# The norm row of q, spread over the partitions by two DMAs through DRAM

## The chip, the core and the metric

The kernel runs on one core of a Trainium2 chip. Its engines work beside each other and meet by semaphores: PE (matmuls; PEld is the load of their weights), DVE (vector), ACT (scalar functions), POOL and SP. SP does nothing here but issue DMAs; POOL issues DMAs and does a little arithmetic. Sixteen DMA engines carry out what both issue; the profile calls SP's queue q1 and POOL's q0. The metric is the device time in microseconds of one execution. Before the change it is 519.28 us, the median of three runs (518.49 to 519.51).

## What is computed

Attention over channels, with each column of q and k divided by its norm, and then a channel mix. B = 4, N = 6208, C = 256, the inner width of the mix is 1024, tau = 1:

```python
qn = q / (np.linalg.norm(q, axis=1, keepdims=True) + 1e-06)
kn = k / (np.linalg.norm(k, axis=1, keepdims=True) + 1e-06)
s = kn.transpose(0, 2, 1) @ qn / tau          # 256 x 256 for each batch
a = softmax(s, axis=-1)
x = v @ a                                     # N x 256
x_prev = x shifted by one row
xk = mu_k * x + (1.0 - mu_k) * x_prev
xr = mu_r * x + (1.0 - mu_r) * x_prev
k = np.maximum(xk @ w_k, 0.0)
out = sigmoid(xr @ w_r) * (k * k @ w_v)
```

The kernel multiplies the raw k and q first and scales the 256 x 256 result: its rows by the inverse norms of k, its columns by the inverse norms of q. A row's factor is one number per partition, which an instruction takes as it is. A column's factor differs along the free dimension and is the same on all partitions: the 256 inverse norms of q have to stand as a row on each of the 128 partitions. This row is what the change is about.

## The kernel before

Batch 0 has a stage of its own at the head (about 40 us). The rest is one pipeline over 48 blocks of 512 rows of v, twelve for each batch, and a last block with the 64 rows that are left of each batch. The outer loop runs over i, from -2 to 48, the inner over j from 0 to 7. One pass of the inner loop is called a slot here, with the number T = 8i + j. Each engine executes its instructions in the order in which the loops emit them; nothing reorders them later. In the steady state a slot emits:

- up(i + 1, j): two matmuls into kT_ps (L336) and the relu on ACT (kr, L339); one slot later DVE squares it (kk, L345)
- down(i, j): three or five matmuls into v_ps (L384); at j = 1 and 5 DVE multiplies a half block with its gate (res, L397), at j = 1 SP stores the block (L400)
- at j = 0, 1, 4, 5 a gate matmul (L355) into the PSUM bank with the tag g, of which there is one; at j = 2 and 6 ACT empties it (L390)
- at j = 0 and 2 x_half(i + 2): x = v @ a for a coming block (L255), which reads a_sb, the softmax of that block's batch, and an ACT copy into X
- at j = 4 the difference delta (L310), at j = 5 and 6 the two halves of xk (L321) for block i + 2, at j = 0 and 1 those of xr
- at j = 1 a DMA transpose of v (vT, L236) on SP, at j = 2 a load of v (L224) on POOL

Beside this, 49 units for each of the batches 1 to 3 are spread over the slots (a table of due slots, `due`). A unit is two matmuls of k with q into s_ps (L423) and a square of the same rows on ACT (L427). take_sum adds squares on DVE (L445, L449); take_norm adds over the partitions with four short matmuls into n_ps (L462), which also lies in bank g, and an ACT copy to ssq (L464). With the last norm of a batch, at j = 7, the pieces of its softmax join the list `chain`, and each slot takes one of them:

- a: the sum of ssq on DVE and the square root on POOL (L163)
- a2: plus 1e-6, and the reciprocal (L168, L170): nrm_o, a tile of 128 x 4, channel p of half h of q at [p, h]
- b1: two DVE products of a diagonal matrix with the inverse norms (dq, L177)
- bcast: an fp32 matmul of ones with dq (L182), which puts the row on all partitions of bank g, and an ACT copy to rq_bc (L492)
- c: s times the row, on DVE (L495)
- e: two exponentials with sums on ACT (L199)
- f: reciprocals and scaling into a_sb on DVE (L203, L204)

A None in the list lets one slot pass. The piece bcast uses bank g, so it is let out at j = 3 or 7 alone, and take_norm is skipped in that slot. By these rules the pieces of batch 1 come at T = 64, 66, 67, 71, 73, 74, 75, and the first x_half that reads the new a_sb at T = 80. The slots of batch 2 are later by 96, those of batch 3 by 192; batch 3 has no units and norms beside its softmax any more.

Batch 0 makes its row with the same functions spread and broadcast, in the stage at the head.

Of the kernel before, what the change touches and what calls it, by code (L numbers as in the profile page):

```python
# [10 lines left out]
F32 = mybir.dt.float32  # L11
# [7 lines left out]
def kernel(  # L19
# [13 lines left out]
    nc = tc.nc  # L33
    B, N, C = q.shape
    D = C
    DF = moe_w_k.shape[1]
    P = 128
# [13 lines left out]
    pq = ctx.enter_context(tc.tile_pool(name="pq", bufs=4))  # L51
    pn = ctx.enter_context(tc.tile_pool(name="pn", bufs=2))
    p2 = ctx.enter_context(tc.tile_pool(name="p2", bufs=3))
    ps = ctx.enter_context(tc.tile_pool(name="ps", bufs=1, space=bass.MemoryType.PSUM))
    ctx.enter_context(tc.manual_schedule())

# [99 lines left out]
    def root(src, n):  # L156
        a = pn.tile([P, 4], F32, name="nrm_a")
        if len(src.shape) == 3:
            nc.vector.tensor_reduce(a[:, :n], src, axis=AX, op=OP.add)
        else:  # L160
            nc.vector.tensor_copy(a[:, :n], src)
        r = pn.tile([P, 4], F32, name="nrm_r")
        nc.gpsimd.tensor_tensor(r[:, :n], a[:, :n], half[:, :n], op=OP.pow)  # L163
        return r

    def inverse(r, n):

        nc.vector.tensor_scalar_add(r[:, :n], r[:, :n], 1e-6)  # L168
        o = pn.tile([P, 4], F32, name="nrm_o")
        nc.vector.reciprocal(o[:, :n], r[:, :n])  # L170
        return o


    def spread(r):
        dq = pn.tile([P, 2, P], F32, name="dq", bufs=1)
        for h in range(2):
            nc.vector.tensor_scalar_mul(dq[:, h], ident_f, r[:, h:h + 1])  # L177
        return dq

    def broadcast(dq, tag, **kw):  # L180
        bc_ps = ps.tile([P, C], F32, name="bc_ps", tag=tag, **kw)
        nc.tensor.matmul(bc_ps, ones_f, dq.rearrange("p h d -> p (h d)"), start=True, stop=True)  # L182
        return bc_ps
# [7 lines left out]
    def soft_half(b, ih, t_sb, rk, e_sb, sm, mx):  # L191

        if SHIFT:
            nc.vector.tensor_scalar_mul(t_sb[:, ih], t_sb[:, ih], rk[:, ih:ih + 1])
            nc.vector.tensor_reduce(mx[:, ih:ih + 1], t_sb[:, ih], axis=AX, op=OP.max, negate=True)
            nc.scalar.activation(e_sb[:, ih], t_sb[:, ih], AF.Exp, bias=mx[:, ih:ih + 1],
                                 accum_out=sm[:, ih:ih + 1])
        else:
            nc.scalar.activation(e_sb[:, ih], t_sb[:, ih], AF.Exp, scale=rk[:, ih:ih + 1],  # L199
                                 accum_out=sm[:, ih:ih + 1])  # L200

    def soft_scale(b, ih, e_sb, sm):
        nc.vector.reciprocal(sm[:, ih:ih + 1], sm[:, ih:ih + 1])  # L203
        nc.vector.tensor_scalar_mul(a_sb[:, b, ih, :], e_sb[:, ih], sm[:, ih:ih + 1])  # L204

    def soft_tiles():
        return (pn.tile([P, 2, C], F32, name="t_sb"), pn.tile([P, 2, C], F32, name="e_sb"),
                pn.tile([P, 2], F32, name="sm"), pn.tile([P, 2], F32, name="mx"))
# [24 lines left out]
    def v_transpose_dma(i):  # L233
        v_bf = st.pop((i, "v"))
        vT = new_vT(i)
        nc.sync.dma_start_transpose(vT.rearrange("p s h t -> p (s h) t"), v_bf.rearrange("p s c -> p (s c)"))  # L236
# [105 lines left out]
    def square(i, fh):  # L342
        m = size(i)
        kr = st.pop((i, "kr", fh))
        nc.vector.tensor_tensor(st[i, "kk"][:, fh, :m], kr[:, :m], kr[:, :m], op=OP.mult)  # L345

    def gate_mm(i, s):
        if s * P >= size(i):
            return
        if s % 2 == 0:  # L350
            st[i, "g", s // 2] = ps.tile([P, 2, D], F32, name="g_ps", tag="g")
        g_ps = st[i, "g", s // 2]
        xr = st[i, "xr"]
        for dh in range(2):
            nc.tensor.matmul(g_ps[:, s % 2], xr[:, dh, s * P:(s + 1) * P], w_r_sb[:, dh, :],  # L355
                             start=s % 2 == 0 and dh == 0, stop=dh == 1, skip_group_check=True)
# [30 lines left out]
    def gate_act(i, u):  # L387

        if (i, "g", u) in st:
            nc.scalar.activation(st[i, "res"][:, 2 * u:2 * u + 2], st.pop((i, "g", u)), AF.Tanh, scale=0.5)  # L390
# [45 lines left out]
    norms = []  # L436
# [38 lines left out]
    def softmax_pieces(b):  # L475
        t_sb, e_sb, sm, mx = soft_tiles()
        hold = {}

        def a():
            hold["n"] = root(ssq[b], 4)  # L480

        def a2():
            hold["r"] = inverse(hold["n"], 4)
            if inv_tau != 1.0:
                nc.vector.tensor_scalar_mul(hold["r"][:, 2:], hold["r"][:, 2:], inv_tau)

        def b1():
            hold["dq"] = spread(hold["r"])

        def bcast():  # L490
            hold["bc"] = pn.tile([P, C], F32, name="rq_bc", bufs=1)
            nc.scalar.copy(hold["bc"], broadcast(hold["dq"], "g"))  # L492

        def c():
            nc.vector.tensor_tensor(t_sb, s_sb[b], hold["bc"].unsqueeze(1).to_broadcast([P, 2, C]), op=OP.mult)  # L495

        def e():
            for ih in range(2):
                soft_half(b, ih, t_sb, hold["r"][:, 2:], e_sb, sm, mx)

        def f():
            for ih in range(2):
                soft_scale(b, ih, e_sb, sm)

        return [a, None, a2, b1, None, bcast, None, c, e, f]


    order = [("q", NB)] + [("q", g) for g in range(LEAD)]
# [71 lines left out]
    chain = []  # L580
    lst = {}

    for i in range(-2, NBLK):
        for j in range(8):
            T = i * 8 + j
            if i == LAST - 1 and j == 7:

                st[LAST, "res"] = pq.tile([P, S, D], F32, name="res", tag="f4", bufs=NF)
                for s in range(2):
                    gate_mm(LAST, s)  # L590
                gate_act(LAST, 0)
            if j in (2, 6):
                gate_act(i, j // 4)
            if 0 <= i + 1 < NBLK:
                up(i + 1, j)
            if j == 0 and i >= 0:
                square(i, 7)
            if j > 0 and 0 <= i + 1 < NBLK:
                square(i + 1, j - 1)
            if j == 5:  # L600
                finish(i, 0)
            if j == 1:
                finish(i - 1, 1)
            if i >= 0:
                if j in (0, 1, 4, 5) and i < LAST:
                    gate_mm(i, j // 4 * 2 + j % 4)
                down(i, j)
            n = i + 2
            if n == 0 and j == 0:
                x_first()  # L610
            if 0 < n < LAST:
                if j == 0:
                    x_half(n, 0)
                if j == 2:
                    x_half(n, 1)
            if n < NBLK:
                if j == 4:
                    mix_delta(n)
                if j in (5, 6) and n > 0:
                    mix(n, "xk", j - 5)  # L620
            if j in (0, 1) and 0 <= i + 1 < NBLK:
                mix(i + 1, "xr", j)
            if j == 7 and 2 <= i + 3 < NPE:
                v_transpose_pe(i + 3, st.pop((i + 3, "v")), 0, S, "v")
            if j == 1 and NPE <= i + 5 < LAST:
                v_transpose_dma(i + 5)
            if j == 2 and NPE < i + 7 < LAST:
                v_load(i + 7)
            bank_g = False
            if chain and (chain[0] is None or chain[0].__name__ != "bcast" or j in (3, 7)):  # L630
                f = chain.pop(0)
                if f is not None:
                    f()
                    bank_g = f.__name__ == "bcast"
            if bank_g:
                pass
            elif j in (3, 7) or j in (2, 6) and len(norms) > 1:
                take_norm()
            if j in (2, 3, 6, 7) or len(sums) > 2:
                take_sum()  # L640
            for u in due.get(T, []):
                b, g, s = units[u]
                at = (b - 1) * (NB + 1) + GORD.index(g)
                more_rows(at + 4)
                unit(b, g, s)
                if g == GORD[-1] and s == S - 1:
                    evac_s(b)
            if i >= 0 and i // NB < B:
                bl = i // NB
                if i % NB == 2 and j == 1:  # L650
                    lst["v"] = left_load(bl)
                if i % NB == 4 and j == 3:
                    lst["t"] = left_transpose(lst["v"])
                if i % NB == 6 and j == 4:
                    left_x(bl, lst["t"])
# [35 lines left out]
```

## Time and profile before

| | |
|---|---|
| median of three runs | 519.28 us |
| the profiled execution | 519.07 us |
| its span, first to last instruction | 517.3 us |
| bc_ps on PE, L182 (three pairs in the pipeline, one at the head) | 380 ns each |
| dq on DVE, L177 | 282 ns each |
| rq_bc on ACT, L492 | 372 ns, three |
| c on DVE, L495 | 685 ns, three |
| e on ACT, L199 | 506 ns each, and 191 for the sum |
| DMA packets | 143202, 83.51 MB |

How to read the profile: the busy share of an engine is an average over the span. A timeline has one line for each instruction, or for some of the same kind in a row: start, duration, engine, source line, operation, what is written and read, and in brackets how long the engine had been idle before it and what it had waited for. Instructions of an engine overlap, so that a matmul of 0.38 us can be followed after 0.22; the distance of starts is what one costs in a full stream. An issue of a DMA says nothing of its end; that is in the DMA view, as the time to landing.

### The profile page before, as it was taken

The numbers are of one execution on the slowest core, as the hardware profiler recorded it, in microseconds if no ns is written. First come the engines' busy times: TensorE is split into PE (matmuls) and PEld (weight loads), VectorE is DVE, ScalarE is ACT, GpSimd is POOL, SyncE is SP. The second block draws the span as 40 slices with busy tenths as digits, with TensorE's granted clock in tenths as the row PEclk, the third lists the DMA queues.
The fourth block names the chain that finished last, engine by engine and source line by source line (L and its number), as shares of the span: only waits on it lengthen the run. The fifth ranks groups of instructions, "written<-read, shape, count | busy, mean of one in ns | idle before, by whom it ended". The sixth has DMA issues, their size and how long they took to land. (4 is left out here: it accounts for less than half of the span.)

```text
span 517.3 us, 10260 instructions
## 1 busy us (share of the span) xinstructions
PE 496.5 (96%) x3770; PEld 340.4 (66%) x3770; DVE 451.2 (87%) x895; ACT 434.7 (84%) x830; POOL 104.1 (20%) x145
## 2 busy tenths in 40 slices
PE   5789899999999999999999999999999999999996
PEld 2464676776667767667666667767666666666675
DVE  3467899999999999999999999999989888888884
ACT  6777899998999899899999899899787777777773
POOL 0036623322341131131251132100031000000000
PEclk9999999999999999999999999999999999999999
DMA  8989999999999999799899999963297653432123
GB/s 311 407 286 185 194 189 205 193 215 169 189 184 194 174 185 148 125 181 168 103 178 214 173 172 153 157 126 81 62 180 130 131 114 88 101 84 80 55 70 101
DMA packets 143202, 83.51 MB, mean 161 GB/s; under 512 B 51184, under 2 KB 139824, under 8 KB 143152
## 3 DMA queue, kind: packets, MB, share of 16 engines
q0 software_dynamic: 65808, 33.01, 52.3%
q1 hardware_dynamic: 77184, 49.72, 38.4%
q8 instruction: 29, 0.48, 0.4%
q10 hardware_dynamic: 160, 0.13, 0.1%
q14 instruction: 21, 0.17, 0.1%
HBM read 78.71 MB, written 25.43 MB: 201 GB/s over the span
## 5 line engine op out<-in xcount | busy, mean ns | idle before, releaser
L339 ACT ACTIVATE kr<-kT_ps 128x512 bf16<-128x512 f32 (+1 forms) x392 | 232.4, 595 | 37.1 <-PE kT_ps L336 29.5
L336 PE MATMUL kT_ps<-xk,w_k_sb 128*128 128x512 bf16 (+1 forms) x784 | 231.3, 377 | 1.1 <-DVE xk L321 1.0
L384 PE MATMUL v_ps<-w_v_sb,kk 128*128 128x256 bf16 x1536 | 230.4, 273 | 0.0
L345 DVE TENSOR_TENSOR kk<-kr 128x512 bf16<-128x512 bf16 (+1 forms) x392 | 162.1, 418 | 36.5 <-ACT kr L339 33.0
L384 PEld LDWEIGHTS <-kk 128*128 128x128 bf16 x1536 | 150.2, 98 | 57.6
L427 ACT ACTIVATE sq<-qk 128x512 f32<-128x512 bf16 (+1 forms) x147 | 93.0, 633 | 1.1 <-DMA qk<-in_k_dram 1.1
L336 PEld LDWEIGHTS <-w_k_sb 128*128 128x128 bf16 x784 | 74.8, 98 | 22.2 <-issue 1.0
L355 PE MATMUL g_ps<-w_r_sb,xr 128*128 128x256 bf16 x388 | 73.8, 272 | 1.2 <-ACT ssq L464 1.1
L257 ACT CAST X<-xT_ps 128x512 bf16<-128x512 f32 x94 | 55.5, 591 | 20.5 <-PE xT_ps L255 19.8
L321 DVE SCALAR_TENSOR_TENSOR xr<-delta,mu_r_t,X 128x512 bf16<-128x512 bf16 x96 | 71.6, 746 | 0.0
L321 DVE SCALAR_TENSOR_TENSOR xk<-delta,mu_k_t,X 128x512 bf16<-128x512 bf16 x94 | 70.2, 746 | 0.0
L355 PEld LDWEIGHTS <-xr 128*128 128x128 bf16 x388 | 37.9, 98 | 48.2 <-issue 4.8
L397 DVE SCALAR_TENSOR_TENSOR res<-res,v_ps 128x512 f32<-128x512 f32 x96 | 65.4, 681 | 0.0
L413 POOL DMA_DIRECT2D qk<-in_q_dram x39 | 28.7, 735 | 164.1 <-ACT sq L427 142.6
L390 ACT ACTIVATE res<-g_ps 128x512 f32<-128x512 f32 x97 | 57.8, 596 | 0.4 <-PE g_ps L355 0.4
L423 PE MATMUL s_ps<-qk 128*128 128x256 bf16 (+1 forms) x294 | 56.1, 272 | 1.7 <-DMA qk<-in_k_dram 1.7
L255 PE MATMUL xT_ps<-vT,a_sb 128*128 128x512 bf16 x188 | 55.9, 379 | 0.2 <-ACT X L282 0.2
L224 POOL DMA_DIRECT2D v_bf<-in_v_dram x48 | 37.3, 779 | 52.4 <-DMA vT<-v_bf 46.9
L445 DVE TENSOR_TENSOR sq<-sq 128x1024 f32<-128x1024 f32 x36 | 43.9, 1220 | 1.0 <-ACT sq L427 1.0
L423 PEld LDWEIGHTS <-qk 128*128 128x128 bf16 (+1 forms) x294 | 26.7, 97 | 14.3 <-DMA qk<-in_k_dram 2.3
L310 DVE TENSOR_TENSOR delta<-X 128x1024 bf16<-128x1024 bf16 x48 | 33.0, 687 | 0.1
L413 POOL DMA_DIRECT2D qk<-in_k_dram x39 | 28.9, 742 | 7.0 <-DMA w_v_sb<-in_moe_w_v_dram 2.1
(72 smaller groups left out, 233.4 us busy)
## 6 DMA issues: line engine op xcount, KB each, us to landing
out_dram<-res SPq DMA_DIRECT2D x48, 512.0 KB, 3.3
v_bf<-in_v_dram POOLq DMA_DIRECT2D x48, 256.0 KB, 8.1
qk<-in_q_dram POOLq DMA_DIRECT2D x36, 256.0 KB, 8.7
qk<-in_k_dram POOLq DMA_DIRECT2D x36, 256.0 KB, 9.3
f<-in_q_dram SPq DMA_DIRECT2D x12, 512.0 KB, 8.5
f<-in_k_dram SPq DMA_DIRECT2D x11, 512.0 KB, 9.3
vT<-v_bf SPq DMA_TRANSPOSE x44, 7.0
w_k_sb<-in_moe_w_k_dram POOLq DMA_DIRECT2D x1, 512.0 KB, 6.0
```

The source lines that it names most:

```text
L255: nc.tensor.matmul(xT_ps, a_sb[:, b, ih, dh * P:(dh + 1) * P], vT[:, :, ih, :], start=ih == 0, stop=ih == 1)
L321: nc.vector.scalar_tensor_tensor(o[:, dh], st[i, "d"][:, dh], mu[:, dh:dh + 1], X[:, dh, c:c + M], op0=OP.mult, op1=OP.add)
L336: nc.tensor.matmul(kT_ps[:, :m], w_k_sb[:, dh, fh * P:(fh + 1) * P], xk[:, dh, :m], start=dh == 0, stop=dh == 1)
L339: nc.scalar.activation(kr[:, :m], kT_ps[:, :m], AF.Relu, scale=RH)
L345: nc.vector.tensor_tensor(st[i, "kk"][:, fh, :m], kr[:, :m], kr[:, :m], op=OP.mult)
L355: nc.tensor.matmul(g_ps[:, s % 2], xr[:, dh, s * P:(s + 1) * P], w_r_sb[:, dh, :], start=s % 2 == 0 and dh == 0, stop=dh == 1, skip_group_ ...
L384: nc.tensor.matmul(v_ps[:, s % 2], kk[:, fh, s * P:(s + 1) * P], w_v_sb[:, fh, :], start=s % 2 == 0 and fh == 0, stop=fh == 7, skip_group_ ...
L390: nc.scalar.activation(st[i, "res"][:, 2 * u:2 * u + 2], st.pop((i, "g", u)), AF.Tanh, scale=0.5)
L397: nc.vector.scalar_tensor_tensor(r, r, 1.0, st.pop((i, "v", u)), op0=OP.add, op1=OP.mult)
L413: nc.gpsimd.dma_start(qk[:rows, :n, i], src_rows(t, b, g))
L423: nc.tensor.matmul(cov[b][:, ih, :], qk[:rows, s, 1, ih * P:(ih + 1) * P], qk[:rows, s, 0, :], start=g == GORD[0] and s == 0 and ih == 0, ...
L427: nc.scalar.activation(G["sq", s // 2][:rows, s % 2], qk[:rows, s], AF.Square)
```

## The change

For batches 1 to 3 the row is no longer made by the diagonal and the matmul. One DMA on SP writes the 256 inverse norms of q from SBUF to a tile in DRAM, and another reads them back, with a stride of 0 over the partitions, into rq_bc. The pieces b1 and bcast are replaced by these two, in successive slots, and eight None stand between the second and c. The rule that held bcast for j = 3 or 7 and skipped take_norm goes with it. By the list, the pieces of batch 1 come at T = 64, 66, 67 (bcast_out), 68 (bcast_in), 77 (c), 78 (e) and 79 (f). The head of the kernel is not touched.

```diff
+    pd = ctx.enter_context(tc.tile_pool(name="pd", bufs=2, space=bass.MemoryType.DRAM))
...
-        def b1():
-            hold["dq"] = spread(hold["r"])
-
-        def bcast():
+        def bcast_out():
+            hold["d"] = pd.tile([2, P], F32, name="rq_d")
+            with nc.allow_non_contiguous_dma(reason="256 words"):
+                nc.sync.dma_start(hold["d"].rearrange("h p -> p h"), hold["r"][:, 0:2])
+
+        def bcast_in():
             hold["bc"] = pn.tile([P, C], F32, name="rq_bc", bufs=1)
-            nc.scalar.copy(hold["bc"], broadcast(hold["dq"], "g"))
+            nc.sync.dma_start(hold["bc"], hold["d"].rearrange("h p -> (h p)").unsqueeze(0).to_broadcast([P, C]))
...
-        return [a, None, a2, b1, None, bcast, None, c, e, f]
+        return [a, None, a2, bcast_out, bcast_in] + [None] * 8 + [c, e, f]
...
-            bank_g = False
-            if chain and (chain[0] is None or chain[0].__name__ != "bcast" or j in (3, 7)):
+            if chain:
                 f = chain.pop(0)
                 if f is not None:
                     f()
-                    bank_g = f.__name__ == "bcast"
-            if bank_g:
-                pass
-            elif j in (3, 7) or j in (2, 6) and len(norms) > 1:
+            if j in (3, 7) or j in (2, 6) and len(norms) > 1:
                 take_norm()
```

## The prediction

> **What bounds the kernel now.** I read the shares of the span first, then the windows around the three places where the row is made, then the timelines of PE, ACT and DVE there, and last the DMA view of the same stretches. The shares, and two windows (columns: PE, PEld, DVE, ACT, POOL busy, clock, DMA share, GB/s):
>
> ```profile
> PE 496.5 (96%) x3770; PEld 340.4 (66%) x3770; DVE 451.2 (87%) x895; ACT 434.7 (84%) x830; POOL 104.1 (20%) x145
> 140.00:165.00 25.00, 24.53 (x184) 16.99 (x183) 24.31 (x51) 22.98 (x49) 10.59 (x14) 1.00 1.26 198
> 165.00:255.00 90.00, 90.00 (x674) 62.57 (x672) 84.97 (x159) 81.74 (x161) 18.79 (x26) 1.00 1.02 156
> ```
>
> PE never rests between the row of batch 1 and that of batch 2 (90.00 of 90), so what PE is spared or made to wait at a row moves the end by as much, if DVE (94% there, 97% at the row) can follow. The timeline at the row of batch 1, PE first, then ACT:
>
> ```profile
> 147.72 0.60 PE L182 MATMUL bc_ps<-dq,ones_f 128*128 128x256 f32 x2
> 148.15 0.38 PE L423 MATMUL s_ps<-qk 128*128 128x256 bf16 x2
> ...
> 153.68 0.59 PE L336 MATMUL kT_ps<-xk,w_k_sb 128*128 128x512 bf16 x2
> 154.75 0.38 PE L355 MATMUL g_ps<-w_r_sb,xr 128*128 128x256 bf16 x2 [0.47 <-ACT ssq L464]
> ...
> 153.57 0.50 ACT L199 ACTIVATE e_sb<-t_sb,nrm_o 128x256 f32<-128x256 f32 x1
> 153.97 0.19 ACT L199 ACTIVATION_READ_ACCUMULATOR e_sb<-t_sb,nrm_o 128x1 f32 x1
> 154.06 0.58 ACT L339 ACTIVATE kr<-kT_ps 128x512 bf16<-128x512 f32 x1
> 154.54 0.16 ACT L464 COPY ssq<-n_ps 128x4 f32<-128x4 f32 x1
> ```
>
> Two losses are seen. The broadcast holds PE from 147.72 to 148.15, 0.43 us. Then the two exponentials (1.0 us of ACT) push back the ssq copy, which must clear bank g before the gate matmul; that starts 1.07 us after the up matmul in front of it, where 0.43 is usual: 0.64 lost. Batch 2 shows both again (265.51; 271.47 to 272.54). Batch 3, with no rows left to sum, differs:
>
> ```profile
> 387.60 0.16 DVE L203 RECIPROCAL sm<-sm 128x1 f32<-128x1 f32 x1 [0.82 <-ACT e_sb L199]
> ...
> 391.25 0.39 PE L336 MATMUL kT_ps<-xk,w_k_sb 128*128 128x512 bf16 x1
> 392.25 0.38 PE L336 MATMUL kT_ps<-xk,w_k_sb 128*128 128x512 bf16 x1 [0.60 <-DVE xk L321]
> ```
>
> DVE waits for the exponentials, its xk comes late, and PE's second matmul starts 1.00 after its first instead of 0.22: 0.78 lost. There too the copy of the row (382.50 to 382.87) holds bank g until 382.92: 0.62 in place of 0.43, 0.19 lost.
>
> **The queues.** SP's timeline, then lines from the DMA view of windows 140.5 to 142 (vT), 150 to 156 (out_dram) and 150.83 to 154.4 (q0):
>
> ```profile
> 141.09 1.69 SPq L236 DMA_TRANSPOSE vT<-v_bf  x1
> 150.83 0.37 SPq L400 DMA_DIRECT2D out_dram<-res  x1
> ...
> vT<-v_bf SPq DMA_TRANSPOSE x1, 8.6
> ...
> out_dram<-res SPq DMA_DIRECT2D x1, 512.0 KB, 7.4
> ...
> q0 software_dynamic: 1409, 0.70, 145.5%
> ```
>
> The transpose lands at 141.09 + 8.6 = 149.7. The store issued at 150.83 has not one packet on q1 until 154.4: POOL's seven loads, issued from 140.86 to 145.31, have the engines to themselves. Elsewhere the same store lands in 3.1.
>
> **What the Trainium skill says.** All on the page "DMA: Bandwidth & Descriptors". "Rules for kernel authors": a non-contiguous last dim makes one descriptor per element, so bcast_out is 256 of 4 bytes. The trace has the like: the two loads of mu (256 words each) fall in window 33 to 34.2, where 500 of 662 packets are under 512 B. "Two DMAs through the same engine are not ordered": the reader has to wait for the writer's semaphore on the issuing engine, so SP stands still between the two. No run here shows that yet. "Anatomy of one DMA": about 2.0 us fixed, mostly the write's receipt, HBM the slowest, plus bytes at 436 GB/s; for 512 KB that makes an estimate of 3.2, and the quiet store shows 3.1. "Queues, rings and completion order": ring order inside a row, and turns between rows packet by packet. The trace agrees on the first (q1 carries the store's packets, then the transpose's) and not quite on the second: the store's first turn came after 3.6 us.
>
> **The change, part by part.** A slot is one pass of the inner loop, T = 8i + j; times are batch 1's.
>
> 1. Removed: per batch two diagonal products on DVE (0.40), one fp32 matmul pair on PE (0.43), one ACT copy (0.27 net) that had waited 0.38 for PE. PE's 0.43 lies on the path. DVE's and ACT's shares lie beside PE and count only as room.
> 2. Moved: take_norm is no longer pushed out of slot 71, so the norm of slot 75 (a pair of short matmuls and the ssq copy) is done at 71, with no exponential near it. c, e, f go from slots 73, 74, 75 to 77, 78, 79. The 0.64 at slot 76 is gone.
> 3. What is late next: x_half of block 12 reads a_sb in slot 80, straight behind f. PE's slot 76 now starts at 153.25, slot 77 at 154.23, slot 80 at 157.70. kr of slot 76 is ready at 153.25 + 0.59 + 0.60 = 154.45; DVE then does kk 0.34, res 0.60, first xk 0.66, and c could start at 156.05, ending by 156.74. The second xk is ready at 157.73; PE asks for it at 157.92, 0.2 to spare. ACT is done with kr of slot 78 at 156.82, with the exponentials at 157.81, the next kr 158.3 and ssq (the norm of slot 79) at 158.5. The gate matmul wanted bank g at 158.13, so a new wait of 0.41. f ends on DVE at 158.95 to 159.0; x_half, pushed by the same wait, wants its second half at 159.31: hidden. Without that cover it would cost 0.3.
> 4. Batches 1 and 2: -0.43 - 0.64 + 0.41 = -0.66 each. Batch 3 by the same steps: -0.43 - 0.19 - 0.78, then c ahead of the second xk costs 0.42 and f ahead of x_half 0.29: -0.69.
> 5. Added on SP: bcast_out (issue 0.43, as mu) at 142.8, behind the transpose in q1, so its packets pass at 149.4. Nobody else needs SP until 150.83; in batch 3 the store and transpose of 384.61 wait some 2 us, which three blocks of lead hide. Landing of bcast_out: no row for words written to DRAM. Lower end 0.3 (the transpose's own tail), upper 3.0 (2.0 fixed by the skill, plus an estimate of 1.0 for 16 slow writes per engine); I take 0.8, since a quiet 512 KB store leaves little room for more: 150.2. bcast_in issues at 150.3; first packet after 3.6 as the store's (0.9 if the queue were quiet): 153.9; 128 packets of 1 KB at the store's rate (105 in 0.8 us) 1.0, landing 0.4: 155.3. c wants it at 156.05. Margin 0.75, cost nothing. If the cover is gone, c stands at the head of DVE, and xk, kk and PE are late by about what is missing. Batch 3: transpose landed 385.8, row out 386.2, issued at 386.3 and back some 2.5 later, between the 1.4 + 0.9 of a quiet queue and the 4.4 that the store of 384.61 takes, at 388.8, c at 389.45.
>
> Sum: 2 x -0.66 - 0.69 = -2.0. Profiled execution: 519.07 (span 517.3 and 1.8 around it) - 2.0 = 517.1. That execution is 0.21 under the median of 519.28, inside the spread of the three, so I leave it.
>
> **Rivals.** A, the row arrives in time: 517.1, from 516.3 (the new waits half as long) to 518.1 (the 0.64 returns at slot 80 and f adds 0.3). For it: the margin above and nine slots between issue and use. Against: PE's seven-tenths per batch hangs on order.
> B, the moved softmax eats the saving: f next to x_half costs 0.6 more per batch, or c is late by some 0.7: 517.1 + 1.8 = 518.9. For it: margins of 0.2 and 0.75 us. Against: DVE has 0.40 + 1.53 less to do ahead of slot 77.
> C, on the other side: the round trip through DRAM misses c. It begins to cost when bcast_out lands later than 151.0 in batch 1, and makes the kernel slower from a total lateness of about 3 us over the three. At the upper end (3.0) bcast_in lands at 157.5, 1.5 late, in batch 3 1.6: 517.1 + 4.6 = 521.7. For it: POOL's burst stands exactly there, and words to DRAM are unmeasured. Against: the store's quick landing.
>
> **Numbers.** About 0.2%, 1.04 us, is what a measurement can tell from no change. A 0.50, B 0.22, C 0.28. Faster: A, 0.50. Same: B and the near edge of C, 0.23. Slower: 0.27. The range reaches from A's low end, a little widened to 516.2, to just short of C's upper end, 521.6; A's own is 516.3 to 518.1.
>
> **What would show it.** L182 on PE once only; PE without a gap at slot 76 and with one of about 0.4 ahead of the gate matmul at slot 80 of batches 1 and 2; bcast_in landing before 156 and 274, and no wait of DVE at L495 on a DMA. Wrong if DVE waits there for rq_bc, if PE waits at L255 for a_sb, or if the row of PE between 165 and 255 is no longer full.

## The result, and the profile after

The changed kernel takes 554.77 us (median of four runs, 552.57 to 558.54) against 519.09 for the kernel before (the three executions above and a fourth): a ratio of 1.0696, with a 95% interval of 1.0631 to 1.0761. It is slower by 7%, where 0.4% faster was forecast; the time lies far outside the stated range of 516.2 to 521.6. The profiled execution has a span of 551.7 us, against 517.3. Two of the runs further down (the order alone, the two rows) had one execution of 1.8 ms each, which their ratios leave out. Line numbers are higher by one to three from here on: c is L498, the write L491, the read L495.

First the page of the kernel after: engines, and the slices of PE and of its granted clock.

```profile
PE 498.4 (90%) x3700; PEld 341.9 (62%) x3764; DVE 452.4 (82%) x889; ACT 434.1 (79%) x827; POOL 103.6 (19%) x145
...
PE   5798999999938999999983999999993999999996
...
PEclk9999999999977999999995999999997999999999
```

The busy times are those of before within 2 us. Nothing has become more work; there are three holes in PE, one for each row, and the clock falls behind each. The view of waits names what was waited for (total, times, longest):

```profile
PE kT_ps L337 <- DVE xk L322: 31.1, 4, 11.1
...
DVE t_sb L498 <- DMA rq_bc<-rq_d: 30.5, 3, 11.2
...
SPq L495 <- DMA rq_d<-nrm_o: 44.5, 3, 15.0
```

DVE stood 30.5 us at c for the row, and PE stood 31.1, nearly all of it for the xk that is queued behind c. On SP the read stood 44.5 us for the write. The row of batch 1 in SP's timeline, and from the DMA view of two windows the times to landing of the transpose ahead of the write, of the write and of the read:

```profile
140.23 1.75 SPq L237 DMA_TRANSPOSE vT<-v_bf  x1
142.07 0.54 SPq L491 DMA_DIRECT2D rq_d<-nrm_o  x1
157.57 0.33 SPq L495 DMA_DIRECT2D rq_bc<-rq_d  x1
```

```profile
vT<-v_bf SPq DMA_TRANSPOSE x1, 9.5
rq_d<-nrm_o SPq DMA_DIRECT2D x1, 1.0 KB, 15.5
...
rq_bc<-rq_d SPq DMA_DIRECT2D x1, 128.0 KB, 8.6
```

The transpose landed at 140.23 + 9.5 = 149.7; the write of 1 KB only at 142.07 + 15.5 = 157.6, 7.8 behind it, and the read at 157.57 + 8.6 = 166.2. DVE and PE at that place:

```profile
154.57 0.75 DVE L322 SCALAR_TENSOR_TENSOR xk<-delta,mu_k_t,X 128x512 bf16<-128x512 bf16 x1
166.16 0.69 DVE L498 TENSOR_TENSOR t_sb<-s_sb,rq_bc 128x512 f32<-128x512 f32 x1 [10.84 <-DMA rq_bc<-rq_d]
```

```profile
156.82 0.38 PE L337 MATMUL kT_ps<-xk,w_k_sb 128*128 128x512 bf16 x1
167.90 0.59 PE L337 MATMUL kT_ps<-xk,w_k_sb 128*128 128x512 bf16 x1 [10.70 <-DVE xk L322]
```

c could have started at 155.32. It waited 10.84 us, and PE 10.70 for the second half of xk. The windows after that (PE, PEld, DVE, ACT, POOL busy, then the granted clock, DMA share, GB/s) show a second price:

```profile
158.00:159.00 1.00, 0.00 (x0) 0.00 (x0) 0.00 (x0) 0.00 (x0) 0.00 (x0) 1.00 0.62 65
160.00:161.00 1.00, 0.00 (x0) 0.00 (x0) 0.00 (x0) 0.00 (x0) 0.00 (x0) 0.50 1.26 157
172.00:173.00 1.00, 1.00 (x7) 0.69 (x6) 0.75 (x2) 1.00 (x3) 0.00 (x0) 0.50 1.08 306
174.00:175.00 1.00, 1.00 (x7) 0.52 (x6) 0.35 (x2) 0.81 (x2) 1.00 (x2) 1.00 1.22 195
```

2.7 us into its pause PE is given half its clock, and it has the whole of it back only 5.7 us after it resumed (2.0 and 4.5 in batch 2, 4.1 and 5.5 in batch 3). The Trainium skill, "TensorE: Matmul & The Clock Gate", section "What's actually happening", says this: half the clock after an idle window of about 3.4 us, the whole after about as long a busy one. The trace agrees on the half. On the times it does not: two of the three drops came sooner and all three returns later, with PE not fully busy before them. Nor does the length of a pause alone decide: in the run with spread words further down a pause of 1.74 us was followed by 3.4 us at half the clock, in the run with pairs one of 2.77 us by none.

And the jam is not SP's alone. The packets of each queue in the window 151 to 157.5 (packets, MB, share of the 16 engines' time), the kernel after, and then the kernel before:

```profile
q0 software_dynamic: 789, 0.39, 177.0%
q1 hardware_dynamic: 3, 0.00, 0.1%
```

```profile
q0 software_dynamic: 1872, 0.93, 106.6%
q1 hardware_dynamic: 594, 0.54, 31.3%
```

While the write has not landed, POOL's loads (q0), which have nothing to do with it, move 0.39 MB in place of 0.93. That SP's queue (q1) moves nothing has another reason: the store that it carried before can't be issued while SP stands still. The 3 packets on q1 are the last of the write. They have started by 151.2, and the write lands 6.4 us later (8.2 and 8.0 us after the last packet in batches 2 and 3). So the words do not spend this time in the queue ahead of the engines, but between the start of their packets and the landing.

### The profile page after: what moved, and what is told of

The parts are those of the page before. It is cut to its first block, busy times and chain, and to the rows that moved or that the text cites. A ratio compares the mean times of both kernels' runs of the same rounds, so it can differ in the third digit from the quotient of the medians.

```text
span 551.7 us, 10180 instructions
## 1 busy us (share of the span) xinstructions
PE 498.4 (90%) x3700; PEld 341.9 (62%) x3764; DVE 452.4 (82%) x889; ACT 434.1 (79%) x827; POOL 103.6 (19%) x145
## 5 line engine op out<-in xcount | busy, mean ns | idle before, releaser
L337 PE MATMUL kT_ps<-xk,w_k_sb 128*128 128x512 bf16 (+1 forms) x725 | 221.1, 379 | 33.1 <-DVE xk L322 31.1
L385 PE MATMUL v_ps<-w_v_sb,kk 128*128 128x256 bf16 x1536 | 233.0, 275 | 0.5
L356 PE MATMUL g_ps<-w_r_sb,xr 128*128 128x256 bf16 x388 | 75.3, 277 | 1.7 <-issue 0.2
L256 PE MATMUL xT_ps<-vT,a_sb 128*128 128x512 bf16 x188 | 57.3, 387 | 0.2 <-ACT X L283 0.2
## 6 DMA issues: line engine op xcount, KB each, us to landing
qk<-in_q_dram POOLq DMA_DIRECT2D x36, 256.0 KB, 10.5
```

The source lines that it names most:

```text
L256: nc.tensor.matmul(xT_ps, a_sb[:, b, ih, dh * P:(dh + 1) * P], vT[:, :, ih, :], start=ih == 0, stop=ih == 1)
L337: nc.tensor.matmul(kT_ps[:, :m], w_k_sb[:, dh, fh * P:(fh + 1) * P], xk[:, dh, :m], start=dh == 0, stop=dh == 1)
L385: nc.tensor.matmul(v_ps[:, s % 2], kk[:, fh, s * P:(s + 1) * P], w_v_sb[:, fh, :], start=s % 2 == 0 and fh == 0, stop=fh == 7, skip_group_ ...
```

## The experiments

Three theories were put against each other. **Words**: writing 256 single words into 1 KB of DRAM is slow in itself. **Queues**: it is late because it stands behind the transpose and in POOL's burst. **Order**: c, e and f in their later slots cost the time, whatever the row does. Ratios are to the kernel before, on the same chip.

### The order alone, and no row at all

The first run is made from the kernel before, the second from the changed one:

```diff
-        return [a, None, a2, b1, None, bcast, None, c, e, f]
+        return [a, None, a2, b1, None, bcast] + [None] * 5 + [c, e, f]
```

```diff
-            nc.vector.tensor_tensor(t_sb, s_sb[b], hold["bc"].unsqueeze(1).to_broadcast([P, 2, C]), op=OP.mult)
+            nc.vector.tensor_tensor(t_sb, s_sb[b], rq_bc0.unsqueeze(1).to_broadcast([P, 2, C]), op=OP.mult)
...
-        return [a, None, a2, bcast_out, bcast_in] + [None] * 8 + [c, e, f]
+        return [a, None, a2] + [None] * 10 + [c, e, f]
```

> The row is made by the diagonal and the matmul as before; only c, e and f stand in slots 77, 78, 79 of the batch as in the change. Theory words (the single-word write to DRAM is what costs): the order is harmless, 518.6 us by the steps of the prediction without the saved matmul and copy (-0.64 + 0.41 in batches 1 and 2, about 0 in batch 3). Theory order (the later slots cost the time themselves): 525 us or more.

> Both DMAs left out, c stays in its new slot and multiplies by the row of batch 0, so the scaling of batches 1 to 3 is left out of the computation. Theory words: 517.1 us, the forecast with a row that costs nothing. Theory order: 525 us or more.

Measured: 518.32 us, ratio 0.9989 (0.9981 to 0.9997), and 516.94 us, ratio 0.9968 (0.9956 to 0.9980). The theory of order falls: neither run is slower than the kernel before (518.85 on that chip), and the second comes within 0.2 us of the forecast for a row that costs nothing. PE's timeline of the second at slot 80 of batch 1:

```profile
157.68 0.59 PE L337 MATMUL kT_ps<-xk,w_k_sb 128*128 128x512 bf16 x2
158.49 0.38 PE L356 MATMUL g_ps<-w_r_sb,xr 128*128 128x256 bf16 x2 [0.22 <-ACT ssq L465]
158.71 0.49 PE L385 MATMUL v_ps<-w_v_sb,kk 128*128 128x256 bf16 x3
159.04 0.59 PE L256 MATMUL xT_ps<-vT,a_sb 128*128 128x512 bf16 x2
```

The gate matmul follows the up matmul after 0.81 us instead of 0.43: a new wait of 0.38, for the ssq copy, and none in front of x_half.

### Single DMAs, on which nothing waits

Made from the kernel before; four of the seven kinds are shown, the others differ in the tile and the piece that is written. The 128 words have the name half_w in the trace.

```diff
+                d = pd.tile([2, P], F32, name=f"near{n}")
+                nc.sync.dma_start(d.rearrange("h p -> p h"), mu_k_t)
...
+                d = pd.tile([2, P, 16], F32, name=f"fara{n}")
+                nc.sync.dma_start(d[:, :, 0].rearrange("h p -> p h"), mu_k_t)
...
+                d = pd.tile([P, 2], F32, name=f"pair{n}")
+                nc.sync.dma_start(d, mu_k_t)
...
+                d = const.tile([P, C], F32, name=f"back{n}")
+                nc.sync.dma_start(d, moe_mu_k.unsqueeze(0).to_broadcast([P, C]))
...
+            if j == 7 and i in probes:
+                probe(probes[i], i)
```

> The kernel before with twelve single DMAs on SP at j = 7 of blocks in the quieter stretches, on which nothing waits: 256 words into 1 KB of DRAM (near), 128 words into 512 B (half), 256 words each 64 B apart (fara) or 512 B apart (farb), 128 pairs of words (pair), two rows of 512 B (rows), and a read of 1 KB onto 128 partitions (back). Theory words: near lands after 8 us or more even here, rows and back after 2 to 4. If it is the neighbourhood of the addresses, fara and farb land in 2 to 4, half and pair in about 5; if it is the count of writes, fara and farb take 8 too. Theory queues (the transpose ahead of it and POOL's burst of loads made it late): all seven land within 4 us.

From the DMA view: KB each, us from issue to landing.

```profile
back<-in_moe_mu_k_dram SPq DMA_DIRECT2D x2, 128.0 KB, 4.7
...
near<-mu_k_t SPq DMA_DIRECT2D x2, 1.0 KB, 13.0
farb<-mu_k_t SPq DMA_DIRECT2D x2, 1.0 KB, 4.7
pair<-mu_k_t SPq DMA_DIRECT2D x2, 1.0 KB, 6.2
...
fara<-mu_k_t SPq DMA_DIRECT2D x1, 1.0 KB, 6.2
half_w<-mu_k_t SPq DMA_DIRECT2D x1, 0.5 KB, 11.5
```

Each kind of write has one landing in this record (rows has none), so the small differences mean nothing; the large one does. The 256 words side by side take 13.0 us, with POOL's loads no denser beside them (0.83 MB in the window 192 to 206) than beside the words 64 B apart (0.67 MB in 207 to 215). The same number of words spread out takes 6.2 and 4.7.

All these times hold the wait for a transpose ahead. Counted from the start of the last packet, the 256 words side by side land after 6.2 us, the 128 words after 4.5, the 128 pairs after 1.5, and the words 64 B apart after 0.8. So it is not the number of small writes but how closely they lie. A plain count of pieces does not order them, though: 128 words and 128 pairs are as many.

### The queue: the write on ACT's

```diff
-                nc.sync.dma_start(hold["d"].rearrange("h p -> p h"), hold["r"][:, 0:2])
+                nc.scalar.dma_start(hold["d"].rearrange("h p -> p h"), hold["r"][:, 0:2])
```

> The change with the write issued on ACT's queue, so that no transpose stands ahead of it; the read stays on SP. Theory words: it lands 8 to 9 us after its issue at about 142, near 151, the read near 158, c waits about 2 us in batches 1 and 2: 520 to 525 us. Theory queues: it lands within 3 us, c does not wait, 517 us.

Measured: 541.0 us, ratio 1.0437 (1.0409 to 1.0464), outside both expectations. A line of the DMA view at batch 1, and one of the waits:

```profile
rq_d<-nrm_o ACTq DMA_DIRECT2D x1, 1.0 KB, 13.2
```

```profile
DVE t_sb L498 <- DMA rq_bc<-rq_d: 19.5, 3, 8.5
```

Without a transpose ahead in its queue the write still takes 13.2, 11.3 and 11.3 us in the three batches, where it took 15.5, 15.6 and 15.2. The change of queue saves c 11 of its 30.5 us and leaves the larger part; my 8 to 9 us for the write was again too little. ACT's queue did not spare it the wait for the engines either: in batch 1 it was issued at 142.6, nearly all of its packets start between 147.5 and 149.6, and it lands at 155.8, again some 6 us after them.

### Is it the wait at c, or the jam?

```diff
         def bcast_in():
-            hold["bc"] = pn.tile([P, C], F32, name="rq_bc", bufs=1)
-            nc.sync.dma_start(hold["bc"], hold["d"].rearrange("h p -> (h p)").unsqueeze(0).to_broadcast([P, C]))
+            pass
...
         def c():
-            nc.vector.tensor_tensor(t_sb, s_sb[b], hold["bc"].unsqueeze(1).to_broadcast([P, 2, C]), op=OP.mult)
+            nc.vector.tensor_tensor(t_sb, s_sb[b], rq_bc0.unsqueeze(1).to_broadcast([P, 2, C]), op=OP.mult)
```

> The write of the 256 words stays where the change has it, the read is left out and c takes the row of batch 0 (the scaling of batches 1 to 3 is left out). Theory wait (all of the loss is c standing for the row, and what PE's clock does in that pause): 517 us, as without any DMA. Theory jam (the write also holds up POOL's loads and SP's transposes so long that PE runs short of rows of q, k or v): 520 to 530 us.

Measured: 516.27 us, ratio 0.9944 (0.9930 to 0.9957). The DMA view at batch 1 shows the same jam:

```profile
v_bf<-in_v_dram POOLq DMA_DIRECT2D x3, 256.0 KB, 16.7
...
rq_d<-nrm_o SPq DMA_DIRECT2D x1, 1.0 KB, 16.6
```

The write lands after 16.6 us, the loads of v around it after 16.7 (9.9 in the kernel before, in its window 140 to 146), and none of that costs anything. So the loss comes through the wait for the row. This run also spares SP its standstill, since there is no read; but in the changed kernel too PE waited for no late load, only 1.3 us in all for rows of q and k (1.7 before).

### The same words further apart, and in pairs

Both are made from the changed kernel. First the words 64 B apart (the lines that fill the tile beforehand and read its first 1 KB are left out here), then the pairs:

```diff
+    far = pd.tile([2, P, 16], F32, name="rq_d", bufs=1)
...
-            hold["d"] = pd.tile([2, P], F32, name="rq_d")
+            hold["d"] = far
...
-                nc.sync.dma_start(hold["d"].rearrange("h p -> p h"), hold["r"][:, 0:2])
+                nc.sync.dma_start(hold["d"][:, :, 0].rearrange("h p -> p h"), hold["r"][:, 0:2])
```

```diff
-            hold["d"] = pd.tile([2, P], F32, name="rq_d")
...
-                nc.sync.dma_start(hold["d"].rearrange("h p -> p h"), hold["r"][:, 0:2])
+            hold["d"] = pd.tile([P, 2], F32, name="rq_d")
+            nc.sync.dma_start(hold["d"], hold["r"][:, 0:2])
...
+            row = hold["bc"].rearrange("q (p h) -> q h p", h=2)
```

> The change with the 256 words written 64 B apart, to a DRAM tile of 16 KB filled once beforehand; the read takes the first 1 KB of it, so the row holds 16 norms and ones, and the scaling of batches 1 to 3 is left out. Theory neighbours (single words that share a short stretch of DRAM hold each other up, and all DMA engines with them): it lands 1 to 2 us behind the transpose, 9 after its issue, the read some 5 to 6 later, c waits up to 1 us per batch: 517 to 520. Theory count (256 small writes are slow wherever they go): 15 us to landing and 545 us or more.

> The change with the two norms of a partition written together, 128 pieces of 8 B into the same 1 KB; the row comes back with the halves interleaved and c reads it with a stride of two, in two instructions. Theory neighbours: fewer pieces share a stretch, 2 to 3 us behind the transpose, c waits 1 to 2 us per batch: 519 to 523. Theory count: half of the pieces, half of the tail, 11 us to landing, c waits 6 to 7: 535 to 540.

Spread words: 520.35 us, ratio 1.0024 (1.0009 to 1.0039). Pairs: 530.83 us, ratio 1.0228 (1.0208 to 1.0247). Batch 1 of each in the DMA view:

```profile
vT<-v_bf SPq DMA_TRANSPOSE x1, 10.5
rq_d<-nrm_o SPq DMA_DIRECT2D x1, 1.0 KB, 10.0
...
rq_bc<-rq_d SPq DMA_DIRECT2D x1, 128.0 KB, 5.1
```

```profile
rq_d<-nrm_o SPq DMA_DIRECT2D x1, 1.0 KB, 10.2
...
rq_bc<-rq_d SPq DMA_DIRECT2D x1, 128.0 KB, 7.1
```

The first is the decisive run: the changed kernel with the same 256 descriptors in the same queue at the same place, and the words further apart. 34 of the 36 us are gone. That the tile had been filled beforehand is not the reason: in the changed kernel batch 3 writes the tile of batch 1 again (the pool has two), and its write took 15.2 us all the same. The spread write lands at 141.66 + 10.0 = 151.7, 1.3 behind the transpose (139.83 + 10.5), in place of 7.8; c waits 2.7 us in all, 1.9 of them in batch 1, which is more than the theory allowed, and the time is just above its range.

The pairs land 1.9 behind their transpose (150.97), as the neighbours theory had it, yet the read takes 7.1 in place of 5.1, and c waits 9.3 in all, so that neither expectation held for the time. All queues together moved 165 GB/s in the 2 us from 152 on, 197 in the run with spread words; a rest of the jam seems to meet the read. That was not taken further.

### Versions that keep the row in time

The pairs with the write on ACT's queue; the same with a2, bcast_out and bcast_in as one piece; and, from the changed kernel, two rows in place of a column:

```diff
-            nc.sync.dma_start(hold["d"], hold["r"][:, 0:2])
+            nc.scalar.dma_start(hold["d"], hold["r"][:, 0:2])
```

```diff
-        return [a, None, a2, bcast_out, bcast_in] + [None] * 8 + [c, e, f]
+        return [a, None, a2_out_in] + [None] * 10 + [c, e, f]
```

```diff
-                nc.sync.dma_start(hold["d"].rearrange("h p -> p h"), hold["r"][:, 0:2])
+            rt_ps = ps.tile([2, P], F32, name="rt_ps", tag="xT")
+            nc.tensor.matmul(rt_ps, hold["r"][:, 0:2], ident_f, start=True, stop=True)
+            rt = pn.tile([2, P], F32, name="rt")
+            nc.scalar.copy(rt, rt_ps)
+            nc.scalar.dma_start(hold["d"], rt)
```

> As the run with pairs, with the write issued on ACT's queue: no transpose ahead of it. It lands 3 to 5 us after its issue near 142, the read is issued by 147 and comes back behind the transpose by 152, c does not wait: 517 us by either theory, unless the write meets POOL's burst, then up to 522.

> As the pairs on ACT's queue, with the write emitted in slot 66 with the reciprocal, one slot earlier. It is issued some 0.5 us earlier; c's wait of 1.1 us in batch 1 becomes 0.6 or less: 517.8 us. If the loads of POOL set when it lands, nothing is gained: 518.4 us.

> The change with the norms turned into two rows of 128 by one fp32 matmul with the identity and an ACT copy, written to DRAM as two pieces of 512 B from ACT's queue. Theory neighbours: no two pieces share a short stretch, it lands 2 to 4 us after its issue, before POOL's burst has filled the queues; the read is issued by 147 and back by 152; c does not wait: 517.6 us (about 0.2 per batch of PE time returns). Theory count predicts the same; theory burst (POOL's loads hold up whatever is issued there): c waits 1 us or more, 519 to 521.

Measured: 518.41 us, ratio 0.9984 (0.9976 to 0.9992); 518.13 us, 0.9989 (0.9977 to 1.0002); 518.17 us, 0.9986 (0.9979 to 0.9992). The first and the last are some 0.15% below the kernel before, with intervals that just leave out 1; the second can't be told from it, or from the first, so the earlier issue is not shown to gain anything. My landing times for all three were too short. The pairs took 7.7 us from ACT's queue, not 3 to 5, and c still waited 1.1 us in batch 1 (1.0 with the earlier issue). With two rows of 512 B the read was issued at 150.17 and not by 147, although nothing stood ahead of the write on its queue; it came back in time, and c did not wait:

```profile
150.17 0.34 SPq L498 DMA_DIRECT2D rq_bc<-rq_d  x1
```

That the loads of POOL delay even a small write there is what fits; none of the runs takes them away.

## Why the prediction was wrong

**Right: steps 1 to 4.** The saving of the matmul, the vanished wait at slot 76, the new one at slot 80 (0.41 forecast, 0.38 measured), f hidden ahead of x_half, and the sum of -2.0: the run without a row stands at 516.94, 1.9 below the kernel before on its chip. The order alone was put at 518.6 and took 518.32. A row of matmuls read from the timelines, with each wait walked through, gave times to a few tenths of a us.

**Wrong: step 5, the landing of bcast_out.** The step says "no row for words written to DRAM", takes 0.8 us from the passing of its packets to the landing, 0.5 behind the landing of the transpose, "since a quiet 512 KB store leaves little room for more", and sets 3.0 as the upper end. Measured: 7.8 behind that landing. The store moves 1 KB pieces; it says nothing on 256 words that lie side by side, and neither does the fixed time that was taken from the Trainium skill, "DMA: Bandwidth & Descriptors". Its section "Anatomy of one DMA" gives that time for DMAs that POOL issues, while this write is SP's. The upper end was that time and a guess at 16 slow writes on each engine, as if it made no difference how closely the words lie. The spread words show that it does: 64 B apart they land 1.3 behind the transpose. The forecast was nearly one for such a write.

**Wrong by the same cause: the read.** 5.0 us forecast (150.3 to 155.3), 8.6 measured in batch 1; with the spread words it was 5.1. From its issue at 157.57 to 162 only POOL's queue has packets in the trace, 0.50 MB: most likely the loads that the jam had held back. In batch 3, which has no loads of q and k left, the read took 4.8. Forecast margin 0.75, less 8.1 by which the write was late against the forecast when counted from its issue (15.5 against 150.2 - 142.8 = 7.4), less 3.6 for the read: 10.95 us of waiting, and 10.84 measured.

**Rival C had the mechanism and not the size.** It named the place, the DVE queue behind c and the xk that PE then lacks, all as measured. Its upper end put the row 1.5 us late. It also counted a us lost for a us waited. In batch 1, from slot 80's gate matmul to the second x_half, PE took 168.56 to 174.15 = 5.6 us in the changed kernel, and 158.49 to 161.64 = 3.15 in the run without a row: 2.4 us more under the halved clock. The same stretch costs 1.9 more in batch 2 and 2.2 in batch 3. With 30.5 of waiting, these 6.5, and less the 2.0 that the rest of the change brings, that makes 35.0; the spans differ by 34.4. The 2.0 has the new waits at slot 80 in it (0.38 in batches 1 and 2 each), which the pause covers in the changed kernel: about the difference.

**Rivals A and B:** the changed kernel met neither. A's 517.1 is what the run without a row shows.

The chance of 0.27 for slower was not the error that mattered. An operation with no row in the trace had been bounded from above by the nearest one that looked like it, and the whole margin was 0.75 us. A bound of 8 us would have made C the larger case.

**What stays open:** what in the write path holds the words up. Runs show that the distance of addresses decides, that POOL's loads suffer with the write, and that the time passes after the words' packets have started; whether it is the number of words in one 64 B stretch, or that several engines write to it, isn't settled, and 128 words (4.5 us after their last packet) against 128 pairs (1.5) speaks against a plain count. It is also open why the read of the pairs took 2 us more than that of the spread words.

## What to carry to other kernels

A transfer that no trace shows has no upper bound from its bytes, and none from a large transfer in the same direction; measure it by itself where nothing waits for it, before an in-order engine is made to stand for it. Don't scatter a column of single words into one small piece of DRAM: make it two rows on the chip first. Setting the words apart helps the write, but reading them back from there was not run. And count the wait of a nearly full PE above its length, for the clock can fall behind it: by some 2 us for each of the three long pauses here, and once already behind a pause of 1.74 us.

## What was not expected of the hardware

- 256 words of 4 B into 1 KB of DRAM: 15.2 to 15.6 us to landing in the changed kernel, 13.0 in the run of single DMAs. The same words 64 B apart: 7.8 to 10.0 in the kernel, 6.2 in the run of single DMAs.
- The words' packets had all started 6.4 to 8.2 us before the write landed, and in the 6.5 us up to the landing in batch 1 POOL's loads moved 0.39 MB where they moved 0.93 before.
- This jam cost the kernel nothing by itself (516.27 us with the write left in and nobody waiting).
- A write of 1 KB in two pieces, alone on its queue, was waited for until 6.2 us after its issue (issued near 144.0, the read at 150.17) while POOL's loads were running.
